# Attention and expert layers on one core: list positions read from DRAM, routing products at half the distance, a third of one expert's list tests on VectorE

## The chip, the cores and the metric

The kernel runs on one core of a Trainium2 chip. The metric is device time in microseconds (us) of one launch. The core has a matrix engine (TensorE, in the rows PE; PEld is its loading of weights), a vector engine (VectorE, DVE), an engine for activations and copies (ScalarE, ACT), GpSimd (POOL), and a queue engine that only issues DMAs (SyncE, SP). Each engine works through its own list of instructions in order and waits on semaphores for the others.

## The reference

Four batches of q, k and v with 5056 rows of 256 columns. The attention runs over the columns: q and k are normed along the rows, a 256 x 256 matrix of scores is made per batch, and v is multiplied with its softmax. The 20224 rows that come out are then routed to eight experts, each of which takes 2528 rows and applies two layers.

```python
qn = q / (np.linalg.norm(q, axis=1, keepdims=True) + 1e-06)
kn = k / (np.linalg.norm(k, axis=1, keepdims=True) + 1e-06)
s = kn.transpose(0, 2, 1) @ qn / tau            # softmax over the last axis
x = (v @ softmax(s)).reshape(20224, 256)
logits = x @ w_gate                             # 8 experts, cap = 2528
for idx in np.argsort(-logits.flatten()):       # greedy: best pair first
    tok, e = idx // 8, idx % 8
    if assigned[tok] < 0 and counts[e] < cap:
        assigned[tok] = e; counts[e] += 1
for e in range(8):
    out[assigned == e] = np.maximum(x[assigned == e] @ w1[e], 0) @ w2[e]
```

## The kernel before

The first 310 us make the scores and the rows x of the attention, which are stored to DRAM (x_d, L302). After that TensorE does the two layers of the eight experts, one after the other: layer1 (L1677) makes a hidden block of up to 512 rows from gathered x, layer2 (L1726) turns it into rows of the output. Every factor is split into a high and a low part, and three products are summed; ScalarE makes the high part (hH, xH), VectorE the low one (hL, xL). Experts 4 to 7 do some blocks with fewer products (layers, L1764). The finished rows are scattered by POOL (L1734), and the rows of the next blocks are gathered by POOL (L1483), moved over DRAM by two kinds of DMA on SP's queue (xr, L1468, and xq, L1473) and turned on VectorE.

Which rows an expert takes is found between the layers. `route` finds the expert that fills first and its threshold: for each digit VectorE tests all keys (L884, for the late experts L704), TensorE adds the counts up over the partitions (L853 and L866, for the late experts L718 or L832), VectorE compares the sums. Then it marks the rows. `compact` turns the marks into the expert's list: `prefix` gives running counts, L1050 passes the counts of the neighbouring partition (rem, L1046), and a tile G of 128 x 2560 holds for each of 20 x 128 list positions a 1 where the position lies behind the partition's first row (L1058). To begin with, G holds the position numbers 0 to 2559, the same in every partition; L1003 writes them on POOL for each expert. L1067 multiplies G with the counts, for three columns of 128 positions at a time, into the PSUM tile pi; then each column is tested against its position number, and the number of smaller entries is summed along the row. For expert 0 ScalarE tests 9 columns and VectorE 11 (L1101); for experts 1 to 5 ScalarE tests all 20 (L1129); for 6 and 7 ScalarE tests 12. From these sums a few small VectorE steps make the row numbers: src, done at L1197, for the gather, and idx, done at L1209, for the scatter.

The order of all this is written out when the kernel is built, by a planner (`Order`). It keeps a planned time for TensorE (`o.pe`) and VectorE (`o.dve`); each product of the layers moves `o.pe` on (`tick`), and after each, `hook` looks which steps of the routing fit. Such a step names its kind: "V" is a VectorE step with its cost, "A" a ScalarE step, which is placed when its input is ready, and "P" a group of TensorE products, which is placed only when its input has been ready for `margin` ns of planned time:

```python
elif eng in "Ppq":
    if eng == "p" or st.ready + (self.margin if eng == "P" else 0) <= self.pe:
        self.pe += cost
        st.mine = st.ready = self.pe + PE_TO_DVE
```

The margin is 0 before the first layers, FIRST_MARGIN (150) in the layers of expert 0, and MARGIN (700) from the layers of expert 1 on (L1888). The planner knows nothing of POOL's work or of waits.

POOL also clears the tile ge (L1216), which the tests of the early experts fill but for one of its 16 slots, before expert 0 is routed. `load_consts` (L518) loads small tables on SP's queue at the beginning.

Of the kernel before, what the change touches and what calls it, by code (L numbers as in the profile page):

```python
# [8 lines left out]
F32 = mybir.dt.float32  # L9
F32R = mybir.dt.float32r  # L10
BF = mybir.dt.bfloat16
I32 = mybir.dt.int32
I16 = mybir.dt.int16
U8 = mybir.dt.uint8
AF = mybir.ActivationFunctionType
OP = mybir.AluOpType
# [5 lines left out]
E, F = 8, 1024  # L22
# [6 lines left out]
COLS = B * NCH * T  # L29
NCOL = -(-CAP // 128)  # L30
# [16 lines left out]
J = 1 << NB  # L47
NT = J - 1
# [23 lines left out]
DVE_TO_PE = 150  # L72
DVE_TO_DVE = 70
EARLY_GAP = 100
MARGIN = 700
FIRST_MARGIN = 150
TURN_LAT = 1150
LAYER_LAT = 1050
# [29 lines left out]
def attention_moe(ctx: ExitStack, tc: tile.TileContext, q, k, vt, tau, wg, w1t, w2t, tabs, out):  # L108
    nc = tc.nc
    V = nc.vector  # L110
    S = nc.scalar
    P = nc.gpsimd
    PE = nc.tensor

    const = ctx.enter_context(tc.tile_pool(name="const", bufs=1))
    dram = ctx.enter_context(tc.tile_pool(name="dram", bufs=1, space=DRAM))
# [31 lines left out]
    V.tensor_scalar(before, jrow, pcol, None, op0=OP.is_gt)  # L148
    follow = const.tile([128, 128], BF, name="follow")
    V.tensor_scalar(follow, jrow, pcol, 1.0, op0=OP.subtract, op1=OP.is_equal)  # L150
    extra = const.tile([128, 1280], F32, name="extra")
    rhalf = const.tile([128, NCOL], F32, name="rhalf")
    V.tensor_scalar(rhalf, jrow[:, 0:NCOL], 128.0, pcol, op0=OP.mult, op1=OP.add)
    V.tensor_scalar(rhalf, rhalf, 0.5, None, op0=OP.add)
# [2 lines left out]
    for lag in range(2):  # L157
# [28 lines left out]
                    op0=OP.mult, op1=OP.add)  # L186
# [4 lines left out]
    for i in range(8):  # L191
        V.tensor_scalar(steps2[:, i], jrow[:, 1:5], float(1 << 14 - 2 * i), -HALF if i == 0 else 0.0, op0=OP.mult,
                        op1=OP.add)
# [110 lines left out]
    with ExitStack() as sctx:  # L304
# [213 lines left out]
        def load_consts():  # L518
            nc.sync.dma_start(wg_t, wg.rearrange("(kb p) e -> p kb e", p=128))
            nc.sync.dma_start(tau_t, tau.to_broadcast([128, 1]))  # L520
            nc.sync.dma_start(U01, tabs[:, 2])

        def load_scale():
            V.reciprocal(scale[:, 0:2], tau_t.to_broadcast([128, 2]))
            V.memset(scale[:, 2:4], 1.0)
# [3 lines left out]
        for b in range(B):  # L529
            todo = {c: [lambda v=v: load_v(*v) for v in LOADS.get((b, c), ())] +  # L530
                    [lambda j=j: job(*j) for j in JOBS.get((b, c), ())] for c in range(NCH)}
            if b == 0:
                def consts():
                    with tc.issue_after(fetched[0].ins):
                        load_consts()

                todo[1] = [consts]
                todo[3] = [lambda: late(load_scale)]
            if b > 0:
                def put(at, fn, b=b):  # L540
                    todo[at].insert(len(LOADS.get((b, at), ())), fn)

                def soft(sb=sb):
                    cur["ac"] = late(softmax, sb, cur["rn"])

                def turn_a():
                    cur["aT"] = late(turned_a, cur["ac"])

                todo.setdefault(SOFT_AT if b == 1 else 0, []).append(soft)
                if b < B - 1:  # L550
                    put(GATES_AT[b - 1], turn_a)
                    if b > 1:
                        put(GATES_AT[b - 1] + 1, lambda b=b: late(gates, b - 1, cur["ac"], cur["aT"]))
                if b == 2:
                    put(0, lambda: late(gates, 0, cur["ac"], cur["aT"]))
            sb, norms = scores(b, todo, norms)
# [25 lines left out]
    def rtile(name, shape=(128, COLS), dt=F32, bufs=None):  # L582
        t = rt.tile(list(shape), dt, name=name, bufs=bufs)
        return t

    def ve(n, rate=1, psum=False, ptr=0):
        return "V", ((120 if psum else 58) + n / rate) / 0.96 + 66 * ptr
# [20 lines left out]
    def route(p, R):  # L608
        nonlocal L, U01, asg, ne, ne2
        r = {}  # L610
# [8 lines left out]
        else:  # L619
# [48 lines left out]
            else:  # L668
# [3 lines left out]
                                op0=OP.mult)  # L672
# [243 lines left out]
            base = rtile("base", (128, 1))  # L916
# [82 lines left out]
            yield ve(COLS)  # L999
            V.tensor_tensor(mk, mk, m2, op=OP.add)  # L1000
            r["mask"] = mk
        r["G"] = rtile("G", (128, NCOL * 128), BF)
        P.iota(r["G"].bitcast(I16), pattern=[[1, NCOL * 128]], base=0, channel_multiplier=0)  # L1003
        yield ve(COLS, 0.5)
        r["sc"] = prefix(r["mask"], "a")
        ei = rtile("ei", (128, 1), I32, bufs=E)
# [3 lines left out]
        routed[p] = r  # L1010
        done["ei", p] = True
        o.add(compact(p), lambda: -1 if p == E - 2 or done.get(("idx", p)) else COMPACT_PRIO)
        if R > 1:
            t2 = rtile("khi")
# [22 lines left out]
    def compact(p):  # L1037
        r = routed[p]
# [17 lines left out]
        G = r["G"]  # L1056
        yield ve(NCOL * 128, 4, ptr=1)
        V.tensor_scalar(G, G.bitcast(I16), first, None, op0=OP.is_ge)  # L1058
        W = COLS + 2
        sgn = rtile("sgn", (128, NCOL))  # L1060
        ext = rtile("ext", (128, NCOL, 2))
        at = rtile("at", (128, NCOL), I32)
        ended = []

        def tested(pi, g0, n):
            for i in range(n):
                PE.matmul(pi[:, i * W:(i + 1) * W], lhsT=G[:, (g0 + i) * 128:(g0 + i + 1) * 128], rhs=E_,  # L1067
                          start=True, stop=True)
# [46 lines left out]
            V.tensor_scalar(at[:, 0:NACT], sgn[:, 0:NACT], 0.5, COLS / 2.0, op0=OP.mult, op1=OP.add)  # L1115
        split = NACT2 if p >= E - 2 else NCOL

        def with_act():
            for g0 in range(0, split, RB):
                n = min(RB, split - g0)  # L1120
                while p >= E - 2 and o.inner:
                    yield "W", 0
                pi = ps_c.tile([128, 512], F32, name="pi")
                yield "P" if p < E - 2 or not g0 else "q", n * 75
                tested(pi, g0, n)
                for i in range(n):
                    yield "A", 600
                    junk = rtile("junk", dt=BF, bufs=2)
                    S.activation(junk, pi[:, i * W:i * W + COLS], AF.Sign, bias=rhalf[:, g0 + i:g0 + i + 1], scale=-1.0,  # L1129
                                 accum_out=sgn[:, g0 + i:g0 + i + 1])  # L1130
                S.activation(ext[:, g0:g0 + n], pi[:, 0:n * W].rearrange("p (i w) -> p i w", w=W)[:, :, COLS:W], AF.Copy)
                yield "A", 200
            ended.append(1)
# [23 lines left out]
        if p >= E - 2:  # L1157
            o.add(with_act(), lambda: -1)
            o.add(with_dve(), lambda: -1)
            while len(ended) < 2:  # L1160
                yield "W", 0
        elif p:
            yield from with_act()
        if p:
            yield ve(NCOL)
            V.tensor_scalar(at[:, 0:split], sgn[:, 0:split], 0.5, COLS / 2.0, op0=OP.mult, op1=OP.add)
        k1 = rtile("k1", (128, NCOL), I32)
        yield ve(NCOL)
        V.tensor_scalar(k1, at, 3, None, op0=OP.bitwise_and)
# [28 lines left out]
        r["src"] = src  # L1198
        r["time"] = o.pe
        done["idx", p] = True  # L1200
        bt = rtile("bt", (128, NCOL))
        yield ve(NCOL)
        V.tensor_scalar(bt, src, float(NCH * CH), None, op0=OP.is_ge)
# [9 lines left out]
    spacer = rt.tile([1, 9], F32, name="spacer")[:, 0:1]  # L1213
    ge = rt.tile([128, COLS // CG, J, CG], BF, name="ge")
    rt.tile([128, 16], F32, name="pad_t")
    P.memset(ge, 0.0)  # L1216
    routed = {}

    class Stream:
# [106 lines left out]
    o = Order()  # L1326
    nphase = [0]

    def plan():
        p = nphase[0]  # L1330
        if p < E and done.get(("start", p)) is None and (p == 0 or done.get(("routed", p - 1))):
            done["start", p] = True

            def job(p=p):
                yield from route(p, E - p)
                done["routed", p] = True
                nphase[0] += 1
            o.add(job(), lambda p=p: 0 if (p == 0 or done.get(("idx", p - 1))) and (
                not done.get(("ei", p)) or done.get(("idx", p))) else EARLY_PRIO)
# [482 lines left out]
    with tc.manual_schedule():  # L1822
# [62 lines left out]
        for p in range(E):  # L1885
            last = p == E - 1
            o.queued = p >= 99
            if p == 1:  # L1888
                o.margin = MARGIN
            def turn_at(c):  # L1890
                return lambda: turn(p, c)
# [74 lines left out]
            if p + 1 in PARTED:  # L1966
                at_end[0] = [cut_more]
                at = LOAD_AT[p in PARTED]
# [67 lines left out]
```

## Time and profile before

| | |
|---|---|
| median of 3 runs | 1292.16 us (1287.87 to 1292.93) |
| the profiled execution | 1292.82 us, span 1291.0 us |
| busy share of the span | PE 96%, PEld 85%, DVE 73%, ACT 50%, POOL 31% |
| stages | scores and x to about 310 us; experts 0 to 7 from 318 us |

The page and the views under it come from one profiled execution. Times count from the first instruction. A group of instructions is named by its line, its engine and operation, and by what it writes and reads (out<-in). "Idle before" is time in which the engine stood still ahead of an instruction, and the name behind the arrow is what came last before it could go; "issue" is time in which the engine waited for nothing that the profile shows. Matrix products are pipelined, so the duration of one is longer than the distance between two.

### The profile page before, as it was taken

How to read it: one execution, taken by the hardware profiler on the slowest of the kernel's cores; microseconds unless marked ns; L12 is line 12 of the kernel's file. 1: busy time of each engine (PE TensorE's matmuls, PEld its weight loads, DVE VectorE, ACT ScalarE, POOL GpSimd, SP SyncE). 2: the span in 40 equal slices, each digit the busy share in tenths (PEclk: the TensorE clock that was granted, in tenths of full speed). 3: DMA queues.
4: the chain of work that ended last, by engine and by line, in shares of the span. 5: the costliest groups of instructions: out<-in, count | busy, mean ns of one | idle time of the engine just before them, and what ended most of it. 6: DMA issues, size and time to landing. Idle time of an engine off the chain costs nothing.

```text
span 1291.0 us, 23586 instructions
## 1 busy us (share of the span) xinstructions
PE 1241.5 (96%) x8710; PEld 1100.8 (85%) x8710; DVE 945.2 (73%) x2396; ACT 644.8 (50%) x1491; POOL 404.6 (31%) x700
## 2 busy tenths in 40 slices
PE   9999999999899999998999999999999999999998
PEld 7888877998788978887989879889889787978798
DVE  6687597888669678767777978787687776665652
ACT  6556652565324344433433745556564655554552
POOL 0000001001523445343444332634335444233422
PEclk9999999999999999999999999999999999999999
DMA  8999884344222154154432642442563443353500
GB/s 318 313 403 400 302 289 154 144 175 175 87 57 83 54 118 137 39 119 98 139 91 73 141 110 72 131 109 64 104 143 109 103 127 104 74 111 106 113 34 32
DMA packets 222515, 179.37 MB, mean 139 GB/s; under 512 B 152384, under 2 KB 193216, under 8 KB 217792
## 3 DMA queue, kind: packets, MB, share of 16 engines
q1 hardware_dynamic: 195328, 98.41, 28.1%
q0 software_dynamic: 17664, 58.22, 13.9%
q10 hardware_dynamic: 9408, 21.24, 4.2%
q8 instruction: 68, 1.11, 0.4%
q14 instruction: 47, 0.39, 0.1%
HBM read 118.06 MB, written 59.77 MB: 138 GB/s over the span
## 4 chain that ended last, share of the span: by engine, by line
PE 67%; issue 14%; POOL 8%; DMA 5%; DVE 3%; ACT 2%; another core or an unknown queue 0%; POOLq 0%; SPq 0%; ACTq 0%; DVEq 0%
PE py L1726 23%; PE ph L1677 22%; PE s L341 8%; PE px L289 8%; POOL out_dram L1734 4%; POOL xg L1483 3%; DMA x_d<-xs 2%; PE pc L853 2%; DMA ua<-in_q_dram 1%; PE px L467 1%; PE ph L1764 1%; DMA uc<-in_k_dram 1%; PE py L1764 1%; DVE hL L1686 1%; PE pi L1067 1%
## 5 line engine op out<-in xcount | busy, mean ns | idle before, releaser
L1726 PE MATMUL py<-uc,hH 128*128 128x256 f32 (+1 forms) x2560 | 339.4, 280 | 3.2 <-issue 3.2
L1726 PEld LDWEIGHTS py<-uc,hH 128*128 128x128 f32 (+1 forms) x2560 | 314.8, 187 | 7.0 <-issue 5.0
L1677 PE MATMUL ph<-xH,ua 128*128 128x512 f32 (+3 forms) x928 | 254.7, 392 | 3.7 <-issue 2.2
L1734 POOL DMA_INDIRECT out_dram<-y,idx x105 | 109.5, 1043 | 373.9 <-ACT y L1731 349.0
L1680 ACT ACTIVATE hH<-ph 128x512 fp32r<-128x512 f32 (+3 forms) x232 | 133.3, 579 | 157.3 <-PE ph L1677 138.3
L1677 PEld LDWEIGHTS ph<-xH,ua 128*128 128x128 f32 x928 | 168.2, 190 | 36.4 <-issue 4.2
L1686 DVE SCALAR_TENSOR_TENSOR hL<-ph,hH 128x512 fp32r<-128x512 f32 (+3 forms) x232 | 153.3, 663 | 52.2 <-ACT hH L1680 39.0
L1726 PE MATMUL py<-uc,hL 128*128 128x256 f32 (+1 forms) x1280 | 181.1, 279 | 1.7 <-issue 1.7
L1483 POOL DMA_INDIRECT xg<-x_d,src x156 | 155.0, 993 | 60.5 <-issue 56.5
L1726 PEld LDWEIGHTS py<-uc,hL 128*128 128x128 f32 (+1 forms) x1280 | 161.4, 187 | 2.2 <-issue 2.1
L1677 PE MATMUL ph<-xL,ua 128*128 128x512 f32 (+3 forms) x464 | 143.2, 388 | 0.0
L1731 ACT ACTIVATE y<-py 128x256 f32<-128x256 f32 (+1 forms) x105 | 40.2, 383 | 163.0 <-PE py L1726 129.0
L1677 PEld LDWEIGHTS ph<-xL,ua 128*128 128x128 f32 x464 | 86.4, 190 | 17.6 <-issue 1.2
L341 PE MATMUL s<-ua 128*128 128x256 f32 x320 | 74.0, 388 | 3.3 <-DMA ua<-in_q_dram 2.0
L341 PEld LDWEIGHTS s<-ua 128*128 128x128 f32 x320 | 60.9, 193 | 15.5 <-issue 6.0
L292 ACT ACTIVATE xs<-px 128x512 f32<-128x512 f32 (+2 forms) x98 | 49.6, 519 | 47.4 <-PE px L289 45.5
L341 PE MATMUL s<-uc 128*128 128x256 f32 x320 | 71.4, 380 | 0.3 <-DMA uc<-in_q_dram 0.3
L341 PEld LDWEIGHTS s<-uc 128*128 128x128 f32 x320 | 60.3, 190 | 9.4 <-issue 1.5
L289 PE MATMUL px<-aH,vh 128*128 128x256 f32 (+1 forms) x232 | 67.7, 294 | 0.5 <-ACT aH L257 0.5
L289 PE MATMUL px<-aH,vl 128*128 128x256 f32 (+1 forms) x232 | 65.8, 284 | 1.4 <-DVE vl L268 1.4
L1734 POOL DMA_INDIRECT out_dram<-c,idx x33 | 34.0, 1030 | 104.2 <-ACT c L1731 101.6
L289 PE MATMUL px<-aL,vh 128*128 128x256 f32 (+1 forms) x232 | 65.7, 284 | 0.0
(431 smaller groups left out, 2178.4 us busy)
## 6 DMA issues: line engine op xcount, KB each, us to landing
x_d<-xs ACTq DMA_DIRECT2D x39, 512.0 KB
xr<-xg SPq DMA_DIRECT2D x34, 512.0 KB
xq<-xr SPq DMA_DIRECT2D x136, 128.0 KB
vr<-in_vt_dram SPq DMA_DIRECT2D x14, 1024.0 KB
uc<-in_k_dram SPq DMA_DIRECT2D x18, 512.0 KB
uc<-in_q_dram SPq DMA_DIRECT2D x18, 512.0 KB
ua<-in_k_dram SPq DMA_DIRECT2D x17, 512.0 KB
ua<-in_q_dram SPq DMA_DIRECT2D x17, 512.0 KB
```

The source lines that it names most:

```text
L289: mm = PE.matmul(px[:, i * C:i * C + width], lhsT=l_, rhs=a_, start=(j == 0), stop=(j == len(terms) - 1))
L292: S.activation(xs[:, t % TH:t % TH + n, 0:width], px[:, 0:n * width].rearrange("p (t c) -> p t c", t=n), AF.Copy)
L341: newest[0] = PE.matmul(sb[:, ib * C:(ib + 1) * C], lhsT=kt[:, t, ib * 128:(ib + 1) * 128], rhs=qt[:, t, :], start=(first and t == 0 and i ...
L853: PE.matmul(D, lhsT=ge[:, g], rhs=oh[:, 0:Q, cs_], start=(g == 0), stop=(g == COLS // CG - 1))
L1483: P.indirect_dma_start(out=xg[:n, i, :], out_offset=None, in_=x_d, in_offset=bass.IndirectOffsetOnAxis(ap=at, axis=0))
L1677: PE.matmul(ph[:, 0:nt], lhsT=l[:, w], rhs=x_[:, kb, 0:nt], start=(i == 0), stop=(i == 5))
L1680: S.activation(hH[:, fb, 0:nt], ph[:, 0:nt], AF.Relu)
L1686: V.scalar_tensor_tensor(hL[:, fb, 0:nt], ph[:, 0:nt], 0.0, hH[:, fb, 0:nt].bitcast(F32), op0=OP.max, op1=OP.subtract)
L1726: PE.matmul(py[:n, 0:C], lhsT=l[:, fb, tk], rhs=w[:, d], start=(j == 0), stop=(j == 23))
L1731: S.activation(y[:n], py[:n, 0:C], AF.Copy)
L1734: sd = P.indirect_dma_start(out=out, out_offset=bass.IndirectOffsetOnAxis(ap=idx[:n, col:col + 1], axis=0), in_=y[:n], in_offset=None)
L1764: PE.matmul(dst, lhsT=w[b][l][:, f], rhs=x[a][i], start=(first and n == 0), stop=(n == 2), skip_group_check=True)
```

## The change

Five edits. A DRAM tensor `ramp` gets the numbers 0 to 2559 once: POOL writes 20 of them into each partition of a small tile, and SP stores the tile. G is no longer written by POOL; `next_ramp` issues a DMA on SP's queue that reads ramp into all 128 partitions of G, for expert 0 before routing starts and for expert p + 1 as soon as expert p's list is made. The clearing of ge is cut to the one slot that the tests don't fill. MARGIN is 350 in place of 700. And expert 1's list has every third of its columns (where the group has three) tested on VectorE, into a tile num, whose six columns are then copied over those of ScalarE's result. The tile extra gives up 16 columns that nothing used, which the small tile takes.

```diff
-MARGIN = 700
+MARGIN = 350
...
-    extra = const.tile([128, 1280], F32, name="extra")
+    extra = const.tile([128, 1264], F32, name="extra")
+    steep = const.tile([128, 32], I16, name="steep")[:, 0:NCOL]
+    P.iota(steep, pattern=[[1, NCOL]], base=0, channel_multiplier=NCOL)
+    ramp = dram.tile([1, NCOL * 128], I16, name="ramp")
...
             nc.sync.dma_start(U01, tabs[:, 2])
+            nc.sync.dma_start(ramp.rearrange("o (p j) -> (o p) j", j=NCOL), steep)
...
-        r["G"] = rtile("G", (128, NCOL * 128), BF)
-        P.iota(r["G"].bitcast(I16), pattern=[[1, NCOL * 128]], base=0, channel_multiplier=0)
+        r["G"] = ramps[p]
...
+        num = rtile("num", (128, NCOL)) if p == 1 else None
+        if p == 1:
+            yield ve(NCOL)
+            V.memset(sgn, 0.0)
...
-                for i in range(n):
+                for i in range(2 if p == 1 else n):
                     yield "A", 600
+                    if p == 1 and i == 1 and n > 2:
+                        less = rtile("junkv", dt=BF, bufs=2)
+                        o.dve = max(o.dve, o.pe) + 370
+                        V.tensor_scalar(less, pi[:, 2 * W:2 * W + COLS], rhalf[:, g0 + 2:g0 + 3], 0.0, op0=OP.is_lt,
+                                        op1=OP.add, accum_out=num[:, g0 + 2:g0 + 3])
...
+            if p == 1:
+                yield ve(NCOL // 3)
+                V.tensor_copy(at[:, 2:NCOL:3], num[:, 2:NCOL:3])
...
         done["idx", p] = True
+        if p + 1 < E:
+            next_ramp(p + 1)
...
-    P.memset(ge, 0.0)
+    P.memset(ge[:, :, NT:J], 0.0)
+    ramps = {}
+
+    def next_ramp(p):
+        ramps[p] = rtile("G", (128, NCOL * 128), BF)
+        nc.sync.dma_start(ramps[p].bitcast(I16), ramp.to_broadcast([128, NCOL * 128]))
+
+    next_ramp(0)
```

## Rows read from the trace of the kernel before

**Rows 1.** The page, busy time and share of the span, instructions.
```profile
PE 1241.5 (96%) x8710; PEld 1100.8 (85%) x8710; DVE 945.2 (73%) x2396; ACT 644.8 (50%) x1491; POOL 404.6 (31%) x700
```

**Rows 2.** Stretches: length, busy time and instructions by engine, clock, DMA share, GB/s.
```profile
456.00:1085.00 629.00, 608.50 (x4344) 543.18 (x4343) 484.54 (x1324) 315.19 (x869) 259.69 (x441) 0.99 0.42 106
```

**Rows 3.** Waits of PE from 456 to 1085 us: total, times, longest.
```profile
PE pc L866 <- DVE Ex L862: 3.7, 3, 2.0
PE pc L718 <- DVE Ec L714: 3.5, 2, 2.9
```

**Rows 4.** Waits of PE in the whole span.
```profile
PE pc L1050 <- DVE rem L1046: 1.8, 2, 1.1
...
PE ph L1677 <- DVE hL L1686: 1.2, 1, 1.2
...
PE pc L853 <- DVE ge L933: 0.5, 1, 0.5
...
PE pc L977 <- DVE tb L974: 0.4, 1, 0.4
```

**Rows 5.** Timeline at expert 1's start: start, duration, instruction, idle before.
```profile
435.82 0.19 DVE L1197 COPY_PREDICATED src<-early,w__5039 128x20 int32<-128x20 int32 x1
...
455.41 0.63 PE L1726 MATMUL py<-uc,hH 128*96 128x256 f32 x4 [0.79 <-issue]
455.87 1.09 PE L1677 MATMUL ph<-xH,ua 128*128 128x512 f32 x4
```

**Rows 6.** One line, L1003: durations in ns (least, median, longest), first and last start.
```profile
L1003 POOL IOTA G<- x8: 2274/2274/2308, 222.8 to 1011.5; 128x2560 int16 x8
```

**Rows 7.** Timeline of DVE beside three of the iotas.
```profile
497.05 2.55 DVE L1046 TENSOR_SCALAR rem<-sc_a 128x160 bf16<-128x160 f32 x1
...
696.16 0.32 DVE L1000 TENSOR_TENSOR tri<-tri 128x160 f32<-128x160 f32 x1
...
981.21 2.29 DVE L969 TENSOR_SCALAR tri<-asg,cs 128x160 f32<-128x160 f32 x1
```

**Rows 8.** One line, L1046.
```profile
L1046 DVE TENSOR_SCALAR rem<-sc_a x8: 293/298/2552, 286.4 to 1015.8; 128x160 bf16<-128x160 f32 x8
```

**Rows 9.** Timeline of SP's queue, a move of 512 KB and those behind it.
```profile
351.15 0.38 SPq L1468 DMA_DIRECT2D xr<-xg  x1
354.09 2.38 SPq L1473 DMA_DIRECT2D xq<-xr  x4
```

**Rows 10.** Timeline of DVE and POOL ahead of the first gather.
```profile
306.63 0.19 DVE L1197 COPY_PREDICATED src<-early,w__3207 128x20 int32<-128x20 int32 x1
...
312.98 1.42 POOL L1483 DMA_INDIRECT xg<-x_d,src  x1 [23.48 <-issue]
```

**Rows 11.** Lines of the list tests, L1101 and (400 to 432 us) L1129.
```profile
L1101 DVE TENSOR_SCALAR_CACHE_REDUCE junkv<-pi,rhalf x11: 373/380/386, 290.5 to 299.3; 128x160 bf16<-128x160 f32 x11
L1101 DVE DVE_READ_ACCUMULATOR junkv<-pi,rhalf x11: 81/83/90, 290.8 to 299.6; 128x1 f32 x11
...
L1129 ACT ACTIVATE junk<-pi,rhalf x20: 384/393/398, 403.4 to 429.2; 128x160 bf16<-128x160 f32 x20
```

**Rows 12.** Stretches, 400 to 425 us.
```profile
400.00:425.00 25.00, 24.68 (x202) 22.00 (x202) 22.10 (x69) 13.26 (x51) 7.91 (x12) 1.00 0.30 106
```

**Rows 13.** Waits of PE from 318 to 402 us.
```profile
PE pc L866 <- DVE Ex L862: 2.1, 3, 1.5
```

**Rows 14.** Lines of routing products, 318 to 402 us, then 456 to 1085 us.
```profile
L866 PE MATMUL pc<-Ex,ones_q x9: 221/225/328, 324.4 to 387.5; 128*128 128x128 f32 x9
...
L866 PE MATMUL pc<-Ex,ones_q x22: 192/220/321, 456.8 to 689.9; 128*128 128x96 f32 x13, 128*128 128x64 f32 x9
...
L718 PE MATMUL pc<-Ec,ones_q x18: 166/170/246, 726.4 to 976.7; 128*128 128x12 f32 x16, 128*128 128x6 f32 x1, 128*128 128x4 f32 x1
...
L832 PE MATMUL pc<-Ec,ones_q x10: 168/168/244, 872.3 to 973.3; 128*128 128x8 f32 x8, 128*128 128x16 f32 x2
```

**Rows 15.** Stretches, behind the wait at L718 of 768.7 us.
```profile
769.99:773.40 3.41, 3.41 (x9) 2.65 (x8) 2.82 (x11) 0.73 (x2) 0.00 (x0) 0.50 0.69 151
```

## The prediction

> **What bounds the kernel now.** I read the busy line of the page first: TensorE (PE) is busy for 96% of the span, VectorE (DVE) for 73%, GpSimd (POOL) for 31% [rows 1]. None of the edits adds or removes a matrix product of the layers or the routing, so whatever the change is worth must come from time in which PE stands still. The view of stretches shows how little that is: from 456 to 1085 us, where the routing of experts 2 to 7 runs between the layers, PE is busy for 608.5 of 629 us [rows 2]. The next view is therefore the list of PE's waits. In that stretch the routing products wait 3.7 us for L862 and 3.5 us for L714 in all [rows 3], and the whole run's list has four entries for DVE work at L1046, L1686, L933 and L974 [rows 4], which I come back to.
>
> Nothing waits for a late list at the start of an expert: from expert 1 on, PE's list has no entry for a gathered x. Expert 1 is the closest. Its list is done at 435.8 and its first product starts at 455.87, right behind the last products of expert 0 [rows 5]. So a routing that ends sooner gives nothing by itself; what counts is how the routing's products and DVE steps disturb PE on the way.
>
> **List positions from DRAM.** Removed: eight POOL iotas of 2.27 us each [rows 6]. POOL is off the path, but the iotas hold DVE. Of the eight, six fall on a DVE tensor_scalar, and that one instruction then lasts about as long as the iota: 2.55 and 2.29 us in the rows shown, while L1046 has a median of 0.298 us [rows 7, 8]. The iota at 696.1 meets a two-input operation, which takes its usual 0.32 us [rows 7]. The Trainium skill, "SBUF — State Buffer", section "Who interferes with whom", states that a DVE instruction in a two-port mode and a GpSimd instruction exclude each other for a whole instruction, and that a DMA never contends with a compute engine. The trace agrees with the first half (2.55 against 0.298 us); no run here yet shows the second, by which the DRAM read would hold no DVE instruction and the term below would come in full.
>
> PE feels the holds in four places, all in one list [rows 4]: 1.8 us at L1050 for rem of L1046 (two times), 1.2 us at L1677 for an hL that stood behind a held L931, 0.5 us at L853 for L933 in the same place, 0.4 us at L977 for tb, behind L969. Sum 3.9 us. Each follows its held instruction within a few us, so I take all of it: **-3.9 us**. Bounds: nothing, if the next input is just as late, and some 3 us more if stops that the list puts down to "issue" beside them go too (0.8 us is one such stop, rows 5).
>
> Added: a 655,360-byte read per expert on SP's queue, and once a 5 KB store behind the first constants, which waits for one short iota at the very start. A 512 KB move takes 2.94 us from its issue to the issue of the moves that wait for it [rows 9], so the read takes some 2.94 x 1.25 = 3.7 us, an estimate. It is issued when the previous list's products have read G; until L1058 needs it, a whole search lies between (for expert 7 only the rest of a list). Behind it on SP stand the xr and xq moves of the next expert, which wait for gathers that come later still. Cost 0; bound +3.7 us once, where it could meet the last stores of x ahead of the first gather (rival C).
>
> **Shorter clearing of ge, first iota gone.** The first iota starts at 222.8 us [rows 6], the clearing stands right before it, both under the last x products. DVE would get some 2 us back in routing expert 0. Its list is done at 306.63, the gather starts only at 312.98, after the last store of x [rows 10]. Hidden by 6 us: 0. No loss can come of it, and no gain either while that store is last.
>
> **Expert 1's columns.** Six of the 20 tests go from ACT, at 0.39 us, to DVE at 0.38 and 0.08 for reading the sum [rows 11]. DVE gets 6 x 0.46 = 2.8 us more between 403 and 429 us. In the planner each ACT step costs 720 ns, so the list ends about 6 x 0.72 = 4.3 us sooner. But PE did not wait for this list [rows 5], so the gain is 0, at best the 0.8 us of issue at 455.41. On the other side DVE is busy for 22.1 of 25 us there [rows 12]; with 2.8 more it has no slack left, and a test is queued ahead of the hL steps, for which the second layer waits. The bound is +2.8 us. I take 0, since a held L1046 goes from the same place and expert 0's list already does eleven such tests on DVE.
>
> **Half the distance.** From expert 1's layers on, a product of the routing is put on PE 350 ns (of planned time) behind its input, not 700. When it waits, the layers stand behind it on PE, in order. The nearest rows: up to expert 1 the distance is 150 (FIRST_MARGIN), and from 318 to 402 us L866 waits 2.1 us in 9 products, 0.23 each; from 456 on, at 700, 3.7 us in 22, 0.17 each [rows 3, 13, 14]. From 700 to 350 is 0.64 of the way from 700 to 150, so 0.64 x 0.06 = 0.04 us more for each. There are 22 L866, 18 L718 and 10 L832 products after 456 [rows 14], 50 in all: **+2.0 us**. L853, ahead of each L866, is left out of the value, its inputs being done earlier. The bounds: with every product of these lines and L853's 22 groups late by the full distance, 72 x 0.35 = +25 us; below, -1 us, since DVE also idles for products and would get its work more evenly. I take +2.0, near the end that has a measured pair.
>
> **Sum.** 1292.8 us (the profiled execution) - 3.9 + 2.0 = 1290.9. That execution lies 0.66 above the median shown, 1292.16, so the forecast for a median is **1290.2 us**; its own range, from the bounds of the small terms, is 1286 to 1295. Half a per cent, 6.5 us, is about what a measurement of this kernel can tell from no change, so this forecast says "no change": faster means under 1285.7, slower over 1298.6.
>
> **Rivals.**
> A, faster: the earlier products also remove waits, because the steps fall elsewhere between the layers. The largest single one is at L718, 2.9 us of the 3.5 [rows 3], where a test on ACT stood behind a copy of y. Right behind it the granted clock is 0.50 for 3.41 us [rows 15], the lower of the two levels (1.2 GHz of 2.4), which gives away 1.7 us of products. If that place is passed and half of L866's 3.7 us go, 2.9 + 1.7 + 1.9 = 6.5 us come off in place of the 2.0 added: 1292.8 - 3.9 - 6.5 - 0.7 = 1281.7. For it: these waits hang on chance neighbours. Against it: a shorter distance makes no input earlier.
>
> B, slower: PE overtakes DVE. With 350 ns the planner has little cover for a DVE step that it underrates or a copy on ACT that is late, and the layers stand behind the product. If 40 of the 72 products find their input late by the whole 0.35, 14.0 us are added: 1292.8 - 3.9 + 14.0 - 0.7 = 1302.2. It decides from (6.5 + 3.9) / 0.35 = 30 late products on; fewer leave the time within half a per cent. For it: 3 of L866's 22 already wait at 700 [rows 3]. Against it: at 150 only 3 of 9 do, for 2.1 us together [rows 13].
>
> C, the iota's work comes back as DMA: the read for expert 1 can start when expert 0's last list products are done, at about 299 us [rows 11], while the last blocks of x are being stored. Were its 3.7 us to lie ahead of the last store, the chain from that store over the gather to the first layer is late by as much: 1290.2 + 3.7 = 1293.9. Against it: 13 us lie between 299 and the gather's start. The Trainium skill's "DMA: Bandwidth & Descriptors", section "Issuing engines are not separate DMA queues", speaks for it: DMAs of all issuing engines run on the same 16 engines and interleave. By that alone the delay could be all of the 3.7 us.
>
> **How the numbers follow.** Forecast 0.45, A 0.33, B 0.16, C 0.06. The forecast's tails give 0.03 to each side. Faster: A and 0.03, 0.36. Slower: B and 0.03, less what of B stays under 30 products (0.02), 0.17. No change: the rest, 0.47. Eight in ten: I leave out the far half of B (0.08) and the part of A that is better than 1280 (0.10): 1280 to 1300.
>
> **What would show it.** In the changed kernel's profile L1046, L931 and L969 should each stay under 0.4 us, and no wait at L1050 for rem should stand in PE's list. L866's waits should be near 0.2 us a product. The list of expert 1 should end some 4 us sooner, and the first product of expert 1 should not move with it. The read should land long before L1058. The prediction is wrong if L866, L718 and L832 together wait for less than half of now (A) or for over 15 us (B), if the first gather starts over 2 us later against the last store (C), or if the entries into later experts turn out to have waited for their lists.

## The result, and the profile after

| | before | after |
|---|---|---|
| median, 8 runs each on one chip | 1292.12 us (1287.87 to 1294.24) | 1301.95 us (1297.47 to 1305.64) |
| ratio, 95% interval | | 1.0071 (1.0051 to 1.0091) |
| profiled execution, span | 1292.82, 1291.0 us | 1303.42, 1301.6 us |
| granted clock, mean over the span | 0.993 | 0.987 |

The change made the kernel slower by 0.7%. The forecast was 1290.2 us and "no change", with 1280 to 1300 as its range. All ratios below are against runs of the kernel before made beside them on the same chip; these had medians of 1292 to 1298 us, but of 1239 to 1240 us for the six kernels marked with a star, and one chip gave both (1297.55 beside m700, 1239.43 beside r650).

The busy line of the page, after (before: [rows 1]):

```profile
PE 1249.1 (96%) x8710; PEld 1106.9 (85%) x8710; DVE 937.8 (72%) x2410; ACT 644.7 (50%) x1479; POOL 381.3 (29%) x693
```

PE runs the same 8710 products and is busy for 7.6 us longer, beside 3.0 us more in which it stands still (1301.6 - 1249.1 against 1291.0 - 1241.5). The 7.6 is mostly clock: 1301.6 x 0.013 = 16.9 us against 1291.0 x 0.007 = 9.0. But this execution had the lowest clock of the eight (0.987 to 0.993), so not all of that share is the change's: the mean of the eight is 0.990, and that of the kernel before is 0.992 in the runs beside m700, early350 and hold7.

The stretch of [rows 2], after, and PE's waits in the whole span, after ([rows 3, 4]; line, what it waited for: total, times, longest):

```profile
456.00:1085.00 629.00, 605.96 (x4294) 540.51 (x4293) 474.05 (x1320) 312.05 (x859) 236.67 (x426) 0.99 0.44 110
```

```profile
PE pc L870 <- DVE Ex L866: 7.2, 6, 4.1
...
PE pc L722 <- DVE Ec L718: 4.7, 5, 2.8
...
PE pi L1070 <- ACT ext L1144: 3.1, 2, 2.5
...
PE pi L1070 <- DVE G L1061: 1.6, 1, 1.6
PE pc L857 <- DVE ge L888: 1.5, 2, 1.3
...
PE pc L836 <- DVE Ec L833: 1.0, 2, 0.6
PE pc L1052 <- DVE cb L1046: 0.8, 1, 0.8
```

The line numbers have moved: L870, L722, L836, L1070 and L1052 are L866, L718, L832, L1067 and L1049 of before, and L1049, L935 and L973 are L1046, L931 and L969. In the stretch PE gets through 50 products fewer. The waits for rem (L1050 before) and for tb are gone; what stands at the head now is few and long: one wait of 4.1 us, one of 2.8, one of 2.5. Behind the two longest the granted clock is at the lower of its two levels, 1.2 GHz of 2.4. The two products, and the stretches around and behind them (the third number from the end is the clock):

```profile
556.57 0.45 PE L870 MATMUL pc<-Ex,ones_q 128*128 128x96 f32 x1 [4.11 <-DVE Ex L866]
...
721.82 0.28 PE L722 MATMUL pc<-Ec,ones_q 128*128 128x12 f32 x1 [2.76 <-DVE Ec L718]
```

```profile
555.00:561.83 6.83, 5.26 (x14) 4.42 (x15) 4.59 (x13) 1.60 (x3) 0.00 (x0) 0.50 0.93 173
722.30:725.71 3.41, 3.41 (x10) 2.67 (x9) 2.91 (x11) 2.69 (x11) 0.00 (x0) 0.50 1.33 182
```

PE is busy for 8.7 us of these at half the speed, which gives away some 4.3 us beside the 6.9 us of the waits themselves.

The edits themselves do what they say. One line each, after: the three instructions that iotas had held (before, 2552, 1992 and 2293 ns at the longest), and the issue of the new read:

```profile
L1049 DVE TENSOR_SCALAR rem<-sc_a x8: 293/298/500, 287.6 to 1007.7; 128x160 bf16<-128x160 f32 x8
...
L935 DVE TENSOR_SCALAR ge<-w,cur x5: 303/303/304, 275.1 to 679.7; 128x160 bf16<-128x160 f32 x5
...
L973 DVE TENSOR_SCALAR tri<-asg,cs x7: 294/295/297, 281.1 to 970.1; 128x160 f32<-128x160 f32 x7
...
L1239 SPq DMA_DIRECT2D G<-ramp x8: 320/344/1712, 221.7 to 1002.9; - x8
```

Expert 1's list, its first product, and the first gather behind the last store of x, after ([rows 5, 10]):

```profile
426.44 0.17 DVE L1213 COPY_PREDICATED src<-early,w__4885 128x20 int32<-128x20 int32 x1
...
456.34 1.09 PE L1702 MATMUL ph<-xH,ua 128*128 128x512 f32 x4
```

```profile
311.48 0.33 ACTq L305 DMA_DIRECT2D x_d<-xs  x1
314.21 1.62 POOL L1508 DMA_INDIRECT xg<-x_d,src  x1 [23.56 <-DMA x_d<-xs]
```

The list is done 9.4 us sooner and the product has not moved. The gather starts 2.73 us behind the last store, against 2.90 before.

And one row that turns out to matter: the first product of expert 7's list, before and after. It comes 26.9 us earlier in the same kernel.

```profile
1034.72 0.18 PE L1049 MATMUL pc<-cb,before 128*128 128x1 bf16 x1
```

```profile
1007.82 0.16 PE L1052 MATMUL pc<-cb,before 128*128 128x1 bf16 x1 [0.80 <-DVE cb L1046]
```

### The profile page after: what moved, and what is told of

Read it like the earlier page. It is cut to its first block, busy times and chain, and to the rows that moved or that the text cites. A ratio compares the mean times of both kernels' runs of the same rounds, so it can differ in the third digit from the quotient of the medians.

```text
span 1301.6 us, 23589 instructions
## 1 busy us (share of the span) xinstructions
PE 1249.1 (96%) x8710; PEld 1106.9 (85%) x8710; DVE 937.8 (72%) x2410; ACT 644.7 (50%) x1479; POOL 381.3 (29%) x693
## 4 chain that ended last, share of the span: by engine, by line
PE 67%; issue 13%; DMA 6%; POOL 6%; DVE 5%; ACT 2%; another core or an unknown queue 1%; SPq 0%; POOLq 0%; ACTq 0%; DVEq 0%
PE py L1751 23%; PE ph L1702 21%; PE s L344 7%; PE px L292 7%; POOL out_dram L1759 3%; DMA x_d<-xs 2%; POOL xg L1508 2%; PE pc L857 2%; DMA ua<-in_q_dram 2%; PE ph L1789 2%; PE py L1789 1%; PE px L470 1%; DMA uc<-in_q_dram 1%; DMA vr<-in_vt_dram 1%; PE pi L1070 1%
## 5 line engine op out<-in xcount | busy, mean ns | idle before, releaser
L1702 PE MATMUL ph<-xL,ua 128*128 128x512 f32 (+3 forms) x464 | 146.7, 392 | 0.0
```

Of the source, the lines that this page charges most:

```text
L1702: PE.matmul(ph[:, 0:nt], lhsT=l[:, w], rhs=x_[:, kb, 0:nt], start=(i == 0), stop=(i == 5))
```

## The experiments

**One edit at a time.** Four kernels, then the two that complete the eight combinations. m700 is the change with `MARGIN = 700`; only_margin, only_ramp and only_e1 are the kernel before with one edit; no_e1 is the change without the tests; e350 is the change without DRAM positions. The ranges in us below were written for a kernel before of 1292 us; beside the first four kernels it took 1297.55, so the ratios are what to compare.

```diff
-MARGIN = 350
+MARGIN = 700        # m700, in the changed kernel
```

> The changed kernel with the distance ahead of routing products put back to 700; DRAM positions and expert 1's tests stay. Theory M (the halved distance is what costs: products of L722, L836 and L870 reach PE before DVE and ACT have their operand, and PE's granted clock falls after the longer of these stalls): 1287 to 1293 us, L870 and L722 wait under 5 us in sum before the last expert, and no more half-speed stretches than the six of before. Theory D (the added DMA read or the tests cost): 1298 to 1304 us. Theory P (any new order of the steps moves the time by up to 10 us, whatever the distance): anything from 1285 to 1305 us, the stalls at other places than in both kernels.

> The kernel before with the distance at 350 and nothing else. Theory M: 1298 to 1306 us (the whole loss of 9.8 us, plus the 2 to 4 us that the positions gain in the changed kernel), with waits of 2 us or more at products of L866 and L718 and some ten half-speed stretches. Theory D: 1290 to 1295 us. Theory P: 1285 to 1305 us, with no tie to the routing products' own waits.

> The kernel before with the positions read from DRAM and the shorter clearing, distance 700, no tests of VectorE for expert 1. My prediction's step: 3.9 us less, 1286 to 1290 us, and no wait of PE at L1050 for rem. Theory D (the 655,360 bytes read meet other transfers): 1293 us or more, with PE waits on DMA queues that before has not. Theory P: 1285 to 1305 us.

> The kernel before with VectorE's tests of a third of expert 1's list columns alone. My prediction's step: nothing, 1291 to 1294 us, expert 1's list done about 4 us sooner and its first product where it was. Theory V (the tests crowd VectorE ahead of the first products of expert 0): 1295 us or more, with new waits of PE for DVE between 400 and 460 us. Theory P: 1285 to 1305 us.

> The changed kernel without VectorE's tests for expert 1: DRAM positions and the distance of 350. If the edits add up (positions 0.30 per cent less, distance 0.45 per cent more): 1.001 to 1.003 of before. If the shorter distance costs more once the positions are read from DRAM: 1.006 to 1.009, the tests of expert 1 free. If the tests and the distance together cost: 1.001 again, and the changed kernel's 1.0071 needs the tests.

> The kernel before with expert 1's tests on VectorE and the distance of 350; positions still written by POOL. If the tests and the distance together cost: 1.009 to 1.011 of before (the changed kernel's 1.0071 and the 0.3 per cent that the positions give). If the edits add up: 1.005. Theory O: anything from 0.996 to 1.009.

| ratio to before | POOL, 700 | POOL, 350 | DRAM, 700 | DRAM, 350 |
|---|---|---|---|---|
| without expert 1's tests | 1 | 1.0045 (1.0028 to 1.0062) | 0.9970 (0.9946 to 0.9993) | 0.9976 (0.9951 to 1.0000) |
| with them | 1.0005 (0.9980 to 1.0030) | 1.0107* (1.0092 to 1.0123) | 0.9975 (0.9954 to 0.9996) | 1.0071 (1.0051 to 1.0091) |

The positions give 0.3%, 3.9 us of 1297.55 (0.9 to 7.0 by the interval). The tests alone show no cost. The short distance has no single price: 0.45% with POOL's iotas, nothing (0.9976 against 0.9970) with DRAM positions, about 1% where the tests are there too (with POOL's iotas this compares a starred kernel with one that isn't). no_e1 lies below all three ranges that were named for it, and e350 in the range for tests and distance together. So theory M in its plain form fell with no_e1; its sign was missing in only_margin too, where no wait at L866 and L718 is longer than 1.3 us. D and V fell with only_ramp and only_e1. What is left to explain is two interplays.

One thing makes the table easier to read. By the profiles TensorE runs its 8710 products in the same order with POOL's iotas as with DRAM positions (before and only_ramp, only_margin and no_e1, only_e1 and m700, e350 and after). The order changes with the distance and with the tests, not with the positions.

**First interplay, distance and iota.** only_margin's profile has it: PE's waits from 985 to 1075 us, then POOL and DVE ahead of the second of them.

```profile
PE py L1726 <- ACT y L1731: 3.1, 1, 3.1
PE pc L1049 <- DVE cb L1043: 2.8, 1, 2.8
```

```profile
1001.87 2.29 POOL L1003 IOTA G<- 128x2560 int16 x1
```

```profile
1001.22 2.99 DVE L1169 TENSOR_SCALAR k<-at 128x20 int32<-128x20 int32 x1
1001.30 2.92 DVE L1172 TENSOR_SCALAR k<-at 128x20 int32<-128x20 int32 x1
1001.38 2.86 DVE L1175 TENSOR_SCALAR k<-at 128x20 int32<-128x20 int32 x1
...
1004.49 0.17 DVE L1181 TENSOR_SCALAR k<-at 128x20 int32<-128x20 int32 x1
...
1005.99 0.15 DVE L1043 CAST cb<-sc_a 128x1 bf16<-128x1 f32 x1
```

With the routing further ahead, expert 7's iota falls on the last steps of expert 6's list, three of which end 2.7 to 2.8 us after they should (a fourth of their kind, L1181, takes 0.17). They start 0.5 to 0.65 us ahead of the iota, while POOL issues a scatter, so not all of this need be the iota's; the spans on POOL are rough. cb stands behind them on DVE and is late for a product that the layers stand behind. e350* has the same: an iota at 971.82, a tensor_scalar of 2.80 us at 971.34, and a wait of 3.4 us for cb. no_e1 has only_margin's order of products and no iota, and there the distance is free: it is the iotas that make it cost 0.45% in only_margin. This one wait is 2.8 of those 5.8 us; the wait for y comes 63 us later, and nothing here ties it to an iota. mh350 tests it in another way, below.

**Where the second one is made.** The change with 350 in the layers of experts 1 to 3 alone, or from expert 4 on alone:

```diff
             if p == 1:
                 o.margin = MARGIN
+            if p == 4:
+                o.margin = 700      # early350; late350 has 700 first, then MARGIN
```

> The changed kernel with the distance of 350 in the layers of experts 1 to 3 only (456 to 860 us) and 700 from expert 4 on. Theory L (the loss is made where late experts are searched, from expert 4's layers on): 1.000 of before or less, near the 0.9975 of the distance 700 with the same other edits. Theory M even (every product pays a little, wherever): half of the 0.96 per cent, 1.002 to 1.003. Theory P (chance places): anything, and the two halves do not add up to the whole.

> The changed kernel with the distance of 700 in the layers of experts 1 to 3 and 350 from expert 4 on. Theory L: 1.005 to 1.008 of before, the whole loss, with waits at L722, L836, L1070 and L1052 after 860 us of 4 us or more in sum. Theory M even: 1.002 to 1.003. Theory P: anything, the halves not adding up.

Measured: early350 1.0067 (1.0041 to 1.0092), late350 0.9991 (0.9969 to 1.0012). Theory L fell, and M even with it: the distance under experts 1 to 3 makes the whole loss, as far as the intervals tell. The halves add up, so P's sign is missing too. Yet early350's profile has the 2.5 us wait at L1070 for ext too, under expert 5, where its distance is 700. So the loss need not lie where the distance is short. Nor is a lead of the routing the loss by itself: expert 7's list begins at 1017.64 us in early350's profile and at 1014.63 in late350's, which loses nothing, against 1041.73 in m700's. What differs is where the list lies against the block named below: late350 makes all of its columns behind the block, early350 has the block in between.

**Is it an accident of one distance?** m650 is the kernel before at 650; a400 and a300 are the change at 400 and 300; r650 is only_ramp at 650.

> The kernel before with a distance of 650 in place of 700: most routing products from expert 1's layers on stand one or a few products of the layers earlier, so the order is another one almost everywhere, while the distance is nearly the same. Theory M even: a seventh of the distance's price, 1.0005 to 1.001 of before, 1297 to 1299 us where before has 1297.5. Theory P: off by more than 0.3 per cent to either side.

> The changed kernel with all three edits and a distance of 400 in place of 350. Theory O (order: the loss comes from where the changed kernel's own order happens to put a dozen products, so a neighbouring distance with another order does not have it): 0.996 to 1.002 of before, stops of over 0.6 us at routing products below 17 us in sum, as in the faster kernels (the changed kernel has 23.0). Theory C (the three edits together cost, at any short distance): 1.005 to 1.008, the stops at 20 us or more.

> The changed kernel with all three edits and a distance of 300. Theory O: 0.996 to 1.003 of before. Theory C: 1.007 to 1.010, a little more than at 350. Both of 300 and 400 near 1.007 would settle it for C, both at 1.002 or less for O.

> The positions from DRAM and the shorter clearing alone, with a distance of 650: the two versions that were faster put together. If their gains add up (0.30 and 0.37 per cent): 0.993 of before, 1286 to 1289 us. Theory O (a distance's worth is the order that it makes in its own kernel and does not carry over): 0.994 to 1.002.

Measured: m650 0.9963 (0.9938 to 0.9989), a400* 1.0054 (1.0040 to 1.0067), a300* 1.0048 (1.0034 to 1.0061), r650* 0.9986 (0.9977 to 0.9995). Small changes of order count, and the loss is still no accident. A change from 700 to 650, which moves many routing products by a few products of the layers, is worth 0.37%, as much as an edit. In r650* that gain did not add to the positions', but its TensorE has no wait left from 318 to 1085 us (last section), so whether the two add where there are waits is open. And 300, 350 and 400 all lose, so the loss isn't an accident of 350, and theory O in that form fell. Theory C got the direction: 400 is in its range, 300 is below it, and the stops of 20 us or more that it named are not there. At L870, L722 and L836, the products that the distance is kept for, a300* waits 0.9 us in all and a400* 1.4, and they lose 0.5% all the same. a400 and a300 share one thing with the change: expert 7's list is cut in two by the block of joined layers (L1789) of expert 5, during which the planner places no step of the routing, and PE waits 2.5 us for ext right behind it (in the changed kernel's profile the block lies from 1019.94 to 1041.81 us; 924, in the expectation of hold7, is near the end of expert 4's).

**The cut list.** hold7 holds expert 7's list until that block is over; split7 cuts it in no_e1, which has it in one piece ahead of the block; nh350 and mh350 do as hold7 in no_e1 and only_margin. Up to that list PE's order is that of the kernel they start from.

```diff
     def compact(p):
+        while p == E - 1 and not done.get(("quad", 5)): yield "W", 0    # hold7, nh350, mh350
...
-                while p >= E - 2 and o.inner:
+                while p >= E - 2 and (o.inner or p == E - 1 and g0 and not done.get(("quad", 5))):    # split7
```

> The changed kernel, expert 7's list products held until the block of joined layers in expert 5 (924 to 1042 us in the changed kernel's profile) is over; on TensorE the order is the same up to that list. Theory S (the torn list is the loss): 0.996 to 0.9995 of before, no wait over 1.2 us at L1070 for ext. Theory C (the three edits cost, wherever the list lies): 1.005 to 1.008 as before.

> The version with DRAM positions and 350, without expert 1's tests (0.9976 of before), with all groups of expert 7's list but the first two held until that block is over; nothing else is moved on TensorE. Theory S: 1.002 to 1.007 of before, some 6 to 10 us more than without the hold, with a wait of some 2.5 us at L1070 for ext. If the torn list costs no more than its own wait: 0.9995 to 1.001. Theory C: 0.9976 again.

> The version with DRAM positions and 350, without expert 1's tests, with the whole of expert 7's list held until that block is over. Theory S: no change from 0.9976, 0.996 to 0.999, since the list lies in one piece either way. If lists ahead of the block are better than behind it: 1.000 or more.

> The kernel before with the distance of 350 and expert 7's list held until that block is over. If the 0.45 per cent of the distance alone were lost at that list too (a wait of 2.8 us at L1049 for cb, then of 3.1 us at L1726 for a copy of y): 0.998 to 1.001 of before. If it is lost all over the search, some 0.05 us at a time: 1.004 to 1.006.

Measured: hold7 1.0079 (1.0051 to 1.0107), split7 0.9990 (0.9967 to 1.0012), nh350 0.9971 (0.9943 to 1.0000), mh350 1.0005 (0.9984 to 1.0026). mh350 agrees with the first interplay: with the list elsewhere nearly all of only_margin's 0.45% comes back. But it does not prove it, since the held list has a wait of its own, 2.7 us at L1067, as long as the one that is gone. And in these runs the cut list is not what costs most in the change: mended, nothing comes back (theory S fell), and made in no_e1 it costs 0.1 to 0.2%, about its own wait and not clear of the noise. hold7 is no clean test of a small share: its list, in one piece, waits 2.9 us at L1070 in place of the 2.5, so some 0.2% could be hidden there. nh350 has that wait too and loses nothing. hold7 and nh350 differ by 13 us in their medians (1305.38 and 1292.43), and by order and tests alone.

**Order or work?** ordA_act keeps the change's PE order to the last product and issues the six tests to ACT; ordN_dve keeps that of no_e1 and issues them to DVE.

```diff
-                        V.tensor_scalar(less, pi[:, 2 * W:2 * W + COLS], rhalf[:, g0 + 2:g0 + 3], 0.0, ...)
+                        S.activation(less, pi[:, 2 * W:2 * W + COLS], AF.Sign, ...)     # ordA_act; ordN_dve the other way
```

> The changed kernel's order of TensorE's work, unchanged to the last product, with the six tests of expert 1 issued to ScalarE in the same places instead of VectorE (with them go the clearing of the sums and the copy of six columns). Theory O (the order is what costs): 1.005 to 1.009 of before. Theory W (the work on VectorE costs): 0.996 to 0.999.

> The order of TensorE's work of the version with DRAM positions and 350 and no tests (0.9976 and, held, 0.9971 of before), unchanged to the last product, with every third test of expert 1 issued to VectorE in the places where ScalarE had it. Theory O: 0.996 to 0.999. Theory W: 1.004 to 1.009. Neither, both near 1.002: order and work pay together.

Measured: ordA_act* 1.0049 (1.0035 to 1.0063), ordN_dve* 1.0003 (0.9991 to 1.0016). Both lie outside theory O's ranges, by 0.0001 and 0.0013, but nearer to them than to W's. The order costs, 5.8 us in the medians (1246.20 and 1240.45), and the six tests on VectorE don't: a400* and a300*, which have them, are no slower than ordA_act, which has not. These 0.46% are half of the 0.95% between no_e1 and the change. Neither of those two was run beside these, so what the other half is isn't shown. Here the two profiles, whose spans are 1244.5 and 1240.7 us, also show where. Busy time by stretch (PE first), ordA_act and then ordN_dve:

```profile
985.00:1050.00 65.00, 61.77 (x410) 55.95 (x409) 46.38 (x88) 39.85 (x92) 25.20 (x47) 1.00 0.49 126
```

```profile
985.00:1050.00 65.00, 65.00 (x427) 58.83 (x425) 45.61 (x83) 37.90 (x76) 28.58 (x53) 1.00 0.52 132
```

ordA_act's PE stands still for 3.2 us here, and for 0.8 more at L1052 ahead of it: 4.0 us, all of the 3.8 by which the two profiled executions differ. Its list in the timeline of PE, and ACT behind the block:

```profile
971.80 0.16 PE L1052 MATMUL pc<-cb,before 128*128 128x1 bf16 x1 [0.80 <-DVE cb L1046]
...
981.77 0.38 PE L1070 MATMUL pc<-E__108,G 128*128 128x162 bf16 x3 [0.31 <-DVE G L1061]
982.28 0.38 PE L1070 MATMUL pi<-E__108,G 128*128 128x162 bf16 x3
...
1003.52 0.38 PE L1070 MATMUL pc<-E__108,G 128*128 128x162 bf16 x3
...
1007.57 0.37 PE L1070 MATMUL pi<-E__108,G 128*128 128x162 bf16 x3 [2.48 <-ACT ext L1143]
...
1016.41 0.37 PE L1070 MATMUL pi<-E__108,G 128*128 128x162 bf16 x3 [0.76 <-ACT ext L1143]
```

```profile
1005.44 0.60 ACT L1813 ACTIVATE hH<-ph 128x512 fp32r<-128x512 f32 x1 [0.84 <-DVE ph L1797]
1005.93 1.14 ACT L1441 ACTIVATE ua<-ub 128x512 fp32r<-128x512 f32 x2
1006.97 0.39 ACT L1141 ACTIVATE junk<-pi,rhalf 128x160 bf16<-128x160 f32 x1
1007.25 0.20 ACT L1141 ACTIVATION_READ_ACCUMULATOR junk<-pi,rhalf 128x1 f32 x1
1007.34 0.17 ACT L1143 ACTIVATE ext<-pi 128x6 f32<-128x6 f32 x1
```

Ten us lie between L1052 and the first list product, because DVE turns gathered x and makes its low parts in between; then the block comes. The group of 1007.57 needs the one PSUM tile pi, which the group of 982.28 still holds: its third test and its copy ext are left for after the block, and stand on ACT behind the block's last copies and the first of the next weights. This product is of the planner's kind "q", which has no distance at all. In ordN_dve DVE does the list first, and all of it is through before the block:

```profile
969.30 0.18 PE L1052 MATMUL pc<-cb,before 128*128 128x1 bf16 x1
971.45 0.38 PE L1070 MATMUL pc<-E__108,G 128*128 128x162 bf16 x3
...
983.88 0.38 PE L1070 MATMUL pi<-E__108,G 128*128 128x162 bf16 x3
984.84 0.64 PE L1787 MATMUL py<-xH,ua 128*128 128x512 f32 x2
```

## Why the prediction was wrong

**List positions from DRAM: right.** -3.9 us was forecast, 0.30% of 1297.55 is 3.9; that the two agree to the tenth is luck, with an interval of 0.9 to 7.0. The held instructions are gone, with their waits, and a read of 640 KB lands 3.8 us behind its issue in ordA_act's profile and 4.1 in ordN_dve's (forecast 3.7). ordA_act's:

```profile
G<-ramp SPq DMA_DIRECT2D x1, 640.0 KB, 3.8
```

In the changed kernel's profile, in the 4 us behind the issue of each of the eight reads, no DVE instruction lasts over 0.24 us longer than the median of its line (the largest: 0.41 us at L1188, where 0.17 is usual). This agrees with the Trainium skill, "SBUF — State Buffer", section "Who interferes with whom", by which a DMA never contends with a compute engine. One rem took 0.50 us, above the 0.4 that was named as a sign, but no read was under way. What the step missed is that an iota's price depends on what it falls on: with the short distance it is 2.8 or 3.4 us of wait at a single place, and then the positions are worth more, 0.7% without the tests (0.9976 against 1.0045) and 0.5 to 0.6% with them (a400* and a300* against e350*, the nearest that were run side by side).

**Clearing, rival C: right.** The gather follows the last store as closely as before. The clearing was not run by itself.

**Expert 1's columns: right as work, wrong as order.** The tests show no cost (1.0005; ordN_dve). Their lead was mis-sized, 7.5 us in place of 4.3: the list ends at 426.07 in m700 and 433.56 in only_ramp (at 426.10 in only_e1 and 435.82 before, 9.7). And "a routing that ends sooner gives nothing by itself" was taken for "does nothing": the search of expert 2 and all steps behind it move with it.

**Half the distance: the step that failed.** It priced products one by one, +0.04 us for each of 50, at the places where they stood before. In the changed kernel's profile that looks not far off: from 456 to 1085 us L870, L722 and L836 wait 4.9 + 4.7 + 1.0 = 10.6 us, 3.2 more than before ([rows 3] and 0.2), and L870 0.22 us a product, where some 0.2 had been named. But this is chance. 4.1 of the 10.6 are a single wait; the same sum is 8.8 us in m700, at the distance of 700, and 5.8 in only_margin at 350, less than the 7.4 of before; and a300* and a400* lose 0.5% with hardly any such wait. So the term does not measure what the distance costs. What the step left out is that a shorter distance puts the whole routing ahead, 26.9 us at expert 7's list, so that steps which have no distance (list products, iotas, the turning of x) meet other neighbours. That was worth between 0 and 1%, by what the other edits had done to the same lead; from m700 to the change (0.9975 to 1.0071) it is some 12 us, where +2.0 had been named. The step also put nothing for the clock behind a wait, which the prediction had read in [rows 15] and used for rival A alone: the 4.3 us above, in this one execution.

**Rival B** named 1302.2 us, nearly the time measured, but not for its reason: not 40 products late by 0.35, but some long waits, and the sum that it set as its sign, over 15 us, was not reached (10.6). The chance of slower, 0.17, was too low because no case in it stood for a changed order.

**What stays open.** For the change itself the cause is open in part. Order is the difference between it and no_e1 as far as ordA_act and ordN_dve carry over, which is for half of the size, and its place isn't settled: all kernels with DRAM positions that lose have the cut list (after, early350, a300, a400, ordA_act) but for hold7, where mending it gave nothing, and split7 has it and shows no loss against before. What early350 shows is only that the loss begins under experts 1 to 3. hold7's profile has more waits of the search from 400 to 860 us than nh350's; the two largest of each, hold7 first:

```profile
PE pc L870 <- DVE Ex L866: 5.4, 3, 4.3
PE pc L722 <- DVE Ec L718: 3.9, 3, 3.0
```

```profile
PE pi L1070 <- ACT ext L1134: 3.9, 1, 3.9
PE pc L722 <- DVE Ec L718: 2.2, 3, 1.3
```

But no_e1, just as fast as nh350, had a 6.4 us stop at L870 in its one profile, so a single profile doesn't price these.

## What to carry to other kernels

In a kernel whose order is written out by a planner, ask of a change of one parameter which steps it moves past which others, above all at the end of the chain that it leads, and not only what each moved step waits for. Measure such a change in combination with the edits that ship with it: here the eight combinations run from 0.997 to 1.011, and no sum of single effects gives the last one. Of the versions tried, m650 (0.9963), only_ramp (0.9970), m700 (0.9975) and r650* (0.9986) lie clear of the kernel before, on the fast side; nh350 (0.9971) and no_e1 (0.9976) have intervals that reach 1.

## What the runs showed of the hardware

The stretch from 318 to 1085 us, only_ramp and then r650*, which differ by 50 ns of distance:

```profile
318.00:1085.00 767.00, 744.38 (x5500) 665.57 (x5501) 576.35 (x1636) 367.53 (x1009) 301.66 (x530) 0.99 0.41 105
```

```profile
318.00:1085.00 767.00, 766.75 (x5755) 695.78 (x5755) 602.87 (x1670) 389.11 (x1047) 313.82 (x558) 1.00 0.43 110
```

r650 has no wait of PE in this stretch; 255 products more fit in. The 50 ns are not the reason: against the kernel before beside them the two are nearly alike (0.9970 and 0.9986). One wait of an unstarred run can be followed back to a result of products that comes late for the engine that waits for it. In the profile of the kernel before, ACT's y waits for products of which the last starts at 763.2 us (six from 762.64) and is recorded as done by 763.49, with the next layer's products behind it:

```profile
762.64 0.85 PE L1726 MATMUL py<-uc,hH 128*128 128x256 f32 x6
763.33 1.10 PE L1677 MATMUL ph<-xH,ua 128*128 128x512 f32 x4
...
768.68 0.25 PE L718 MATMUL pc<-Ec,ones_q 128*128 128x12 f32 x1 [2.86 <-DVE Ec L714]
```

```profile
767.13 0.38 ACT L1731 ACTIVATE y<-py 128x256 f32<-128x256 f32 x1 [3.87 <-PE ph L1677]
```

ACT stands for 3.87 us, its tests and with them Ec are late, and the product at L718 waits 2.86: this is the largest single wait of [rows 3]. The prediction named the test that stands behind the copy; the copy itself was late. How many waits begin like this, and why the result comes late, no run here shows.
